# Another order for a fused attention and feed-forward kernel's written-out list of steps

## The chip, the cores and the metric

The kernel runs on one core of one Trainium2 chip. The metric is device microseconds of an execution; the figure for a kernel is the median of several runs. One further execution was recorded by the hardware profiler, and its durations are the ones used here.

## What is computed

Sliding-window attention with a linear distance penalty feeds a feed-forward layer. Cut to what matters:

```python
# q, k, v: 8 batches x 8 heads x 576 positions x 64
scores = q @ k.T / sqrt(64) - slope[h] * |i - j|     # only where 0 <= i - j < 128
attn   = exp(scores - max) / sum                     # per row
x      = (attn @ v)  ->  4608 tokens x 512
h      = x @ w_in                                    # 512 x 2048
out    = (h * sigmoid(beta * h)) @ w_out             # 2048 x 512, float32 out
```

## The kernel before

Everything lives in one function. It allocates its buffers, defines one small function for each kind of step, and then walks through one string, `PLAN` (line 18 on), of 1,300 words. Each word is a step: a name, sometimes a dot and the engine that does it (`p` GpSimd, called POOL in the profile; `v` VectorE, DVE; `a` ScalarE, ACT; `s` the SyncE queue, SP), and numbers. The loop at the end (lines 716 to 719) calls the function for each word in order:

```python
for step in PLAN.split():
    name, *at = step.split(":")
    name, _, eng = name.partition(".")
    STEPS[name](*([ENGINES[eng]] if eng else []), *map(int, at))
```

So the list is a written-out order of the program. Every engine and every queue executes its own instructions strictly in the order in which the list has them; between engines only semaphores hold, for data and for buffers that are reused. Nothing reorders afterwards. Whether two neighbours of the list on different engines run at the same time is decided when they run.

The work comes in 8 batches of 576 tokens (five blocks of 128, 128, 128, 128 and 64 rows) for attention and in 9 groups of 512 tokens for the feed-forward layer. The steps that matter here:

- `k`, `q` (line 315) and `gk`, `gq`, `gv` (line 306) load float32 inputs by SP into one of 14 staging buffers (`fst`). A load reuses a buffer, so it also waits for the cast that read it.
- `ck`, `cq`, `cK`, `cQ`, `cv` cast such a buffer to bf16 (all on line 205, `move`), into `bst` (4 buffers) or, for v, straight into the matmul operand `vs`. From batch 3 on v comes by a casting DMA of POOL, `pv` (line 342).
- `w1:n` and `w2:n` (lines 350 and 354) load a quarter of each weight matrix by POOL's casting DMA: `w2:n` brings rows 512n to 512n+511 of `w_out`.
- Batches 0 and 1: `Rk`, `Rq` transpose on TensorE (line 369), `rk`, `rq` copy the result out of PSUM, `A`, `B` are scores (lines 410 and 421), `EA`, `EB` exponentials (line 431), `VA`, `VB` the products with v (line 453), `nA`, `nB` the division (lines 437 and 438), `XP` the transposition for the next layer (line 464), `xc` its copy. `z` is an idle matmul (line 209), `fr`, `ft`, `fl` build constants.
- Batches 2 to 7: `D:b:s` (line 500) transposes block s of q and k by a DMA of SP into `qkT`; `S:b:m:p` are scores (line 522; half m = 0 needs blocks 0 to 2, half 1 all five), `E` the exponential (line 531), `M` the mask factor (lines 261 and 275), `V:b:s` the product with v (lines 574 and 577), `n` the division (lines 585 and 586), `XD` (line 620) the transposing DMA of SP that writes `XT`, the input of the next layer.
- `H:g:j` (line 632; in pieces `h`) is column block j of the first matrix product of group g, four matmuls of 512 columns into one bank of PSUM; `a:g:j` (line 640) its activation on ScalarE, `d:g:j` (line 645) the gating product on VectorE, which frees the bank and writes `gT`.
- `O:g:i:n` (line 655) is a quarter of the second product for 128 tokens, four matmuls; quarter n reads `w2:n` and columns 4n to 4n+3 of `gT`. `oc` (lines 677 and 679) evicts the result, `st` (line 684) stores it. The very last 128 tokens go in two halves (`OL` line 666, `lc`, `ls`).

The last number of each TensorE step is one of the 8 PSUM banks, so the list also decides which earlier result must have been evicted before a step can start.

Of the kernel before, what the change touches and what calls it, by code (L numbers as in the profile page):

```python
# [18 lines left out]
k.s:0:2 const ck.a:0:2 k.s:0:0 k.s:0:1 q.s:0:0 beta:4 k.s:1:0 ck.p:0:0 cq.v:0:0 ones ck.a:0:1 z:2:2  # L19
q.s:0:1 ck.a:1:0 z:2:1 q.s:0:2 q.s:0:3 Rk:0:0:3 Rk:0:1:6 z:1:4 z:1:2 k.s:1:3 gv.s:0:1 k.s:0:3  # L20
cq.v:0:1 Rk:0:2:0 Rk:1:0:1 rk.a:0:0 Rq:0:1:2 cq.v:0:2 rq.a:0:1 Rq:0:2:3 q.s:1:0 q.s:1:1 ck.p:1:3
ck.p:0:3 rq.a:0:2 rk.v:0:1 rk.v:0:2 Rq:0:0:4 B:0:1:6:0 rk.v:1:0 rq.a:0:0 B:0:0:4:0 A:0:2:2:1 EB:0:1
MB:0:1 cv.p:0:1 fr:2 cq.v:1:0 cq.a:0:3 A:0:0:6:1 EB:0:0 EA:0:2 z:2:0 gv.s:0:0 EA:0:0 B:0:2:0:1
cv.p:0:0 Rk:0:3:5 MB:0:0 fr:6 A:0:1:2:1 Rq:0:3:4 Rk:1:3:6 rq.v:0:3 rk.a:0:3 B:0:3:4:1 EA:0:1 EB:0:2
cq.v:1:1 EB:0:3 w1:0 Rq:1:1:7 rk.v:1:3 VA:0:0:3 VA:0:1:0 Rq:1:0:2 VA:0:2:6 A:0:3:4:1 nA:0:0 order
rq.v:1:1 gv.s:0:3 rq.a:1:0 cv.p:0:3 gv.s:0:2 B:1:0:1:0 k.s:1:1 q.s:1:3 cv.p:0:2 w1:1 nA:0:1 nA:0:2
VB:0:2:7 EA:0:3 VB:0:3:5 nB:0:2 ck.a:1:1 VB:0:1:4 VB:0:0:3 Rk:1:1:0 A:1:0:6:1 EB:1:0 nB:0:0 cq.p:1:3
q.s:1:2 nB:0:1 cq.p:1:2 rk.a:1:1 k.s:1:2 EA:1:0 XP:0:2:3 XP:0:0:2 w1:2 VA:0:3:4 gq.s:0:4 xc.a:0:0
nB:0:3 nA:0:3 Rq:1:3:1 XP:0:1:0 xc.v:0:2 A:1:1:5:1 rq.a:1:3 XP:0:3:1 pad ck.p:1:2 EA:1:1 A:1:3:3:1
B:1:1:6:0 xc.a:0:1 xc.a:0:3 h:0:0:5:0:3 EB:1:1 fr:7 fr:5 fr:4 EA:1:3 MB:1:0 H:0:2:1 gv.s:1:2  # L30
h:0:0:5:3:4 h:0:1:7:0:3 H:0:3:2 Rq:1:2:3 h:0:1:7:3:4 Rk:1:2:6 MB:1:1 a:0:2 a:0:3 d:0:2 fr:3 gv.s:1:1
fr:1 rk.v:1:2 a:0:0 H:0:7:1 gv.s:0:4 gk.s:0:4 H:0:6:4 H:0:4:6 gv.s:1:0 d:0:3 d:0:0 fr:0 cQ.a:0:4
fl:0 a:0:7 rq.a:1:2 cv.p:1:2 A:1:2:2:1 a:0:6 d:0:7 a:0:4 H:0:10:5 gv.s:1:3 H:0:5:0 gk.s:1:4 a:0:1
H:0:8:1 d:0:6 EA:1:2 d:0:4 a:0:10 w1:3 a:0:5 ft cK.p:0:4 cv.p:0:4 d:0:1 cv.p:1:0 a:0:8 cv.a:1:1
B:1:2:2:1 d:0:10 EB:1:2 H:0:9:5 VA:1:2:6 gq.s:1:4 d:0:5 d:0:8 gv.s:2:4 gv.s:2:1 gk.s:2:0 VA:1:0:1
TT:0:7 H:0:11:4 cv.p:1:3 a:0:9 VA:1:1:0 a:0:11 nA:1:2 tt.v:0 nA:1:0 d:0:9 B:1:3:6:1 EB:1:3 VB:1:2:5
SCT:0:1 nA:1:1 w2:0 VB:1:0:0 gv.s:1:4 gq.s:2:0 VA:1:3:3 d:0:11 ECT:0 gk.s:2:1 cK.p:2:1 VB:1:1:4
gk.s:2:2 cv.p:1:4 H:0:14:7 nB:1:2 nB:1:1 h:0:15:1:0:2 cQ.a:1:4 gq.s:2:4 gk.s:2:4 a:0:14 cK.a:1:4
VB:1:3:4 w2:1 h:0:15:1:2:4 XP:1:1:2 nA:1:3 MCT:0 PV:0:0:6 nB:1:0 XP:1:2:3 PV:0:1:5 gq.s:2:2 cQ.p:2:2
xc.a:1:1 d:0:14 XP:1:0:0 xc.a:1:0 xc.a:1:2 TT:1:2 nV:0:1 nV:0:0 nB:1:3 a:0:15 H:0:12:7 H:0:13:0  # L40
tt.v:1 w2:2 X:0:4:3 a:0:13 XP:1:3:4 x.v:0:4 d:0:13 xc.a:1:3 SCT:1:5 H:1:7:2 ECT:1 a:1:7 H:1:14:0
d:0:15 a:0:12 fl:2 d:1:7 H:1:9:6 H:1:12:1 a:1:12 d:0:12 gq.s:2:1 gq.s:2:3 d:1:12 H:1:3:4 H:1:5:5
H:1:4:1 a:1:3 a:1:9 H:1:1:3 H:1:10:2 a:1:5 d:1:3 H:1:0:7 a:1:4 a:1:14 d:1:4 w2:3 a:1:1 a:1:10
cK.v:2:2 O:0:0:0:4 d:1:5 d:1:14 d:1:1 cQ.v:2:0 cQ.p:2:1 cv.p:2:4 d:1:10 cK.v:2:0 D:2:0 d:1:9
H:1:15:0 H:1:2:1 gq.s:3:1 D:2:2 a:1:2 a:1:0 H:1:13:5 cv.v:2:1 cQ.a:2:4 O:0:2:0:2 H:1:6:3 O:0:2:1:2
H:1:8:6 O:0:0:1:4 O:0:0:2:4 d:1:0 a:1:6 a:1:13 cK.a:2:4 gk.s:2:3 D:2:1 d:1:2 d:1:13 MCT:1 d:1:6
gv.s:2:0 O:0:2:2:2 O:0:3:0:3 gq.s:3:0 H:1:11:7 a:1:8 a:1:15 a:1:11 d:1:8 cQ.v:2:3 cv.p:2:0 d:1:15
gk.s:4:0 cQ.p:3:1 cK.v:2:3 d:1:11 O:0:0:3:4 O:0:2:3:2 O:0:3:1:3 D:2:4 D:2:3 S:2:0:0:0 S:2:0:1:5
oc.v:0:2 O:1:0:0:2 O:1:0:1:2 gv.s:2:3 E:2:0:1 E:2:0:0 gk.s:3:4 st.s:0:2 O:0:3:2:3 S:2:0:2:6 oc.v:0:0
S:2:0:3:4 PV:1:1:0 gk.s:3:0 E:2:0:3 O:1:0:2:2 E:2:0:2 gq.s:3:2 nV:1:1 fl:4 gv.s:2:2 M:2:0:3 M:2:0:2  # L50
O:0:3:3:3 fl:3 oc.v:0:3 S:2:1:3:4 E:2:1:3 M:2:0:1 fl:1 S:2:1:2:0 S:2:1:0:6 E:2:1:0 O:1:0:3:2
oc.a:1:0 M:2:1:3 E:2:1:2 S:2:1:1:4 M:2:0:0 gq.s:3:4 cv.p:2:2 cQ.v:3:0 M:2:1:0 O:0:1:0:3 E:2:1:1
PV:1:0:6 O:0:1:1:3 gq.s:4:1 gk.s:3:2 gk.s:4:4 gq.s:3:3 V:2:0:0 nV:1:0 cQ.p:3:4 M:2:1:2 O:1:1:0:2
V:2:1:4 n:2:0 O:1:2:0:7 gk.s:3:1 O:1:2:1:7 n:2:1 cQ.p:3:2 M:2:1:1 O:1:1:1:2 X:1:4:6 XD:2:0 XD:2:1
cv.a:2:3 pv:3:1 V:2:2:0 n:2:2 XD:2:2 O:1:2:2:7 O:1:1:2:2 V:2:3:4 O:1:2:3:7 x.a:1:4 cK.v:3:4
O:0:1:2:3 cK.v:3:0 n:2:3 oc.a:1:2 O:0:1:3:3 O:1:1:3:2 cK.v:3:2 cK.v:3:1 gk.s:3:3 st.a:0:0 V:2:4:5
H:2:4:0 H:2:1:7 D:3:0 D:3:2 n:2:4 gq.s:4:2 H:2:10:4 a:2:1 a:2:4 oc.a:0:1 D:3:1 oc.v:1:1 gk.s:4:2
H:2:3:1 H:2:5:6 d:2:4 H:2:2:0 d:2:1 H:2:0:7 D:3:4 a:2:5 H:2:7:3 st.s:1:0 a:2:10 d:2:10 a:2:2 a:2:3
cQ.p:4:1 a:2:0 a:2:7 gq.s:4:0 cK.p:3:3 cQ.v:3:3 d:2:2 d:2:5 d:2:3 H:2:9:4 O:1:3:0:2 a:2:9 cQ.p:4:0
S:3:0:0:5 S:3:0:2:0 O:1:3:1:2 d:2:0 d:2:7 gk.s:5:4 D:3:3 st.a:0:1 O:1:3:2:2 E:3:0:0 E:3:0:2  # L60
S:3:0:1:6 d:2:9 S:3:0:3:3 H:2:6:5 gk.s:4:1 H:2:11:1 O:1:3:3:2 H:2:8:0 E:3:0:1 pv:3:2 E:3:0:3 a:2:6
S:3:1:1:6 a:2:11 a:2:8 XD:2:3 H:2:12:4 E:3:1:1 d:2:6 d:2:11 cK.p:4:2 pv:3:0 cQ.v:4:2 a:2:12 H:2:13:5
d:2:8 M:3:0:1 d:2:12 oc.v:1:3 cK.p:4:0 S:3:1:0:0 E:3:1:0 H:2:14:6 M:3:0:3 M:3:0:2 S:3:1:3:3 a:2:14
S:3:1:2:0 d:2:14 E:3:1:3 O:2:0:0:2 O:2:0:1:2 E:3:1:2 D:4:0 gq.s:4:3 H:2:15:7 M:3:1:3 st.p:0:3
cK.p:4:1 pv:3:4 M:3:0:0 cQ.p:4:3 pv:4:0 st.p:1:2 a:2:15 a:2:13 M:3:1:1 M:3:1:0 d:2:15 O:2:2:0:3
O:2:0:2:2 pv:3:3 V:3:0:0 O:2:1:0:6 n:3:0 cK.v:4:4 d:2:13 M:3:1:2 O:2:1:1:6 V:3:1:0 n:3:1 O:2:1:2:6
V:3:2:4 O:2:1:3:6 n:3:2 gk.s:4:3 D:4:1 D:4:2 gq.s:4:4 gk.s:5:3 cK.v:4:3 cQ.p:4:4 O:2:0:3:2 O:2:2:1:3
st.a:1:1 oc.a:2:1 S:4:0:1:6 pv:4:1 S:4:0:3:4 S:4:0:2:0 E:4:0:1 O:2:2:2:3 E:4:0:3 O:2:3:0:7 E:4:0:2
XD:2:4 XD:3:0 XD:3:2 XD:3:1 oc.v:2:0 D:4:4 D:4:3 O:2:2:3:3 V:3:3:4 V:3:4:0 n:3:3 O:2:3:1:7 oc.v:2:2
O:2:3:2:7 n:3:4 H:3:2:4 H:3:0:2 a:3:2 S:4:0:0:5 d:3:2 a:3:0 gq.s:5:2 gq.s:5:0 M:4:0:1 H:3:7:0  # L70
E:4:0:0 d:3:0 a:3:7 O:2:3:3:7 H:3:1:5 d:3:7 oc.a:2:3 a:3:1 S:4:1:2:2 S:4:1:0:0 M:4:0:2 st.s:2:0
cQ.p:5:2 S:4:1:1:6 gk.s:5:1 E:4:1:0 d:3:1 E:4:1:1 H:3:6:4 H:3:4:5 a:3:6 E:4:1:2 H:3:3:1 XD:3:4
M:4:0:3 M:4:0:0 V:4:0:6 H:3:9:0 a:3:4 d:3:6 n:4:0 V:4:1:3 gq.s:5:1 XD:3:3 H:3:5:2 gk.s:5:2 pv:4:2
st.s:1:3 gq.s:5:3 H:3:12:7 gq.s:7:4 gk.s:5:0 XD:4:0 cK.a:5:1 a:3:3 n:4:1 a:3:9 M:4:1:0 H:3:8:3
XD:4:1 d:3:4 a:3:8 S:4:1:3:5 H:3:15:4 cK.p:5:2 E:4:1:3 d:3:3 pv:4:3 pv:4:4 a:3:12 d:3:9 H:3:14:0
a:3:14 a:3:5 d:3:8 pv:5:1 M:4:1:2 d:3:14 d:3:5 H:3:10:3 H:3:11:1 H:3:13:5 a:3:10 a:3:13 gq.s:5:4
H:4:1:2 H:4:4:6 H:4:2:0 cQ.p:5:3 a:3:11 cK.a:5:0 cQ.a:5:1 M:4:1:3 d:3:12 d:3:13 O:3:1:0:5 H:4:0:7
cQ.v:5:0 d:3:11 a:4:1 cK.p:5:3 cQ.p:5:4 D:5:2 a:3:15 st.s:2:1 a:4:2 gq.s:6:2 a:4:0 d:3:10 D:5:0
d:4:1 d:4:2 cK.v:5:4 gk.s:6:0 D:5:1 d:4:0 a:4:4 O:3:1:1:5 H:4:7:1 H:4:3:0 M:4:1:1 d:3:15 d:4:4 a:4:7
pv:5:4 H:4:5:7 a:4:3 O:3:0:0:4 O:3:0:1:4 O:3:1:2:5 V:4:4:2 a:4:5 O:3:1:3:5 d:4:3 d:4:7 d:4:5  # L80
S:5:0:1:6 S:5:0:0:0 st.s:2:3 gk.s:7:1 n:4:4 D:5:4 D:5:3 gk.s:6:2 V:4:2:2 E:5:0:1 oc.v:3:1 n:4:2
O:3:0:2:4 E:5:0:0 gq.s:7:2 V:4:3:6 n:4:3 O:3:0:3:4 S:5:0:2:2 E:5:0:2 pv:6:1 S:5:1:0:0 pv:5:0 XD:4:4
gk.s:7:0 oc.a:3:0 pv:5:2 S:5:0:3:5 st.a:3:0 E:5:1:0 gq.s:6:4 st.p:2:2 H:4:6:7 O:3:2:0:3 O:3:3:0:2
O:3:2:1:3 st.p:3:1 E:5:0:3 S:5:1:1:4 S:5:1:2:0 E:5:1:1 a:4:6 O:3:3:1:2 O:3:2:2:3 E:5:1:2 M:5:0:0
M:5:0:2 M:5:0:3 M:5:0:1 V:5:0:4 O:3:3:2:2 XD:4:2 gq.s:6:3 O:3:3:3:2 n:5:0 V:5:1:5 XD:5:0 H:4:8:1
XD:4:3 O:3:2:3:3 a:4:8 n:5:1 oc.a:3:2 H:4:9:5 a:4:9 oc.a:3:3 H:4:11:6 H:4:10:3 H:4:12:2 d:4:8
M:5:1:2 d:4:9 a:4:11 a:4:12 d:4:11 d:4:6 H:4:13:1 H:4:15:4 XD:5:1 a:4:15 a:4:10 O:4:1:0:7 H:4:14:5
a:4:14 a:4:13 O:4:1:1:7 d:4:12 cQ.v:6:2 d:4:10 d:4:15 gk.s:6:1 d:4:13 gq.s:6:1 gk.s:6:4 gq.s:7:0
d:4:14 H:5:2:0 a:5:2 M:5:1:1 d:5:2 H:5:8:2 H:5:10:3 H:5:1:5 O:4:1:2:7 S:5:1:3:0 a:5:8 d:5:8 cK.a:6:2
# [660 lines left out]
```

## Time and profile before

| what | value |
|---|---|
| runs | 323.64, 324.43, 325.98 us; median 324.43 |
| the profiled execution | 323.59 us |
| its span, first to last instruction | 321.8 us |
| granted TensorE clock, mean over the span | 0.994 |
| busy, ScalarE and VectorE | 58% and 62% |
| DMA: read from HBM, written to it | 36.71 MB, 9.44 MB |
| last matmul ends | 318.3 us |

A line of a timeline has the start, the time it took, the engine (SPq is SP's queue of DMA issues), the line of the code, what is written and read and how many instructions it merges; in square brackets stands the idle time before it and what ended it. A line of the stretches has the stretch, its length, and for TensorE, its weight loads, VectorE, ScalarE and POOL the busy time with the number of instructions, then the granted clock, the busy share of the DMA engines and GB/s. A line of the waits has the waiting engine and line, what it waited for, the sum in us, how often, and the longest.

### The profile page before, as it was taken

The page shows a single profiled execution, that of the slowest core. Times are in us where ns is not written, and L with a number is a line of the kernel's source. Part 1 is how long each engine was busy: PE and PEld are TensorE (multiplying, and loading weights), DVE is VectorE, ACT ScalarE, POOL GpSimd, SP SyncE. Part 2 cuts the span into 40 slices and gives each one's busy share as a digit, 9 for nine tenths or more (in the row PEclk, how much of TensorE's full clock was granted, in tenths as well). Part 3 has the DMA queues.
Part 4 walks back from the last instruction along what each step waited for, and adds up shares of the span by engine and source line. Part 5 has one row for each costly group of instructions (what it writes and reads, how often), then busy time and mean ns, then how long its engine had stood idle before and what let it go on. Part 6 is the DMA issues. An engine that isn't in the chain of part 4 may idle for free.

```text
span 321.8 us, 5879 instructions
## 1 busy us (share of the span) xinstructions
PE 307.9 (96%) x2218; PEld 152.2 (47%) x2257; DVE 198.1 (62%) x391; ACT 186.3 (58%) x278; POOL 62.9 (20%) x101
## 2 busy tenths in 40 slices
PE   8899999979989999899999999999999999999995
PEld 3464554434544445354455444544544544444543
DVE  4789886843856494588755645752876536865102
ACT  7999786615407854479565664746469324773010
POOL 2372404101301631242050143112000000000000
PEclk9999999998999999999999999999999999999999
DMA  7999999999999999999999899599651134000023
GB/s 243 281 250 199 194 202 187 180 210 223 201 167 233 189 201 172 202 226 179 210 152 230 149 178 138 71 174 182 84 103 35 51 70 152 1 33 2 33 83 147
DMA packets 152684, 50.01 MB, mean 155 GB/s; under 512 B 140288, under 2 KB 148752, under 8 KB 152656
## 3 DMA queue, kind: packets, MB, share of 16 engines
q1 hardware_dynamic: 122512, 37.24, 63.2%
q0 software_dynamic: 28384, 9.51, 27.4%
q10 hardware_dynamic: 1760, 2.89, 2.5%
q8 instruction: 17, 0.28, 0.4%
q14 instruction: 11, 0.09, 0.1%
HBM read 36.71 MB, written 9.44 MB: 143 GB/s over the span
## 4 chain that ended last, share of the span: by engine, by line
PE 74%; DMA 12%; SPq 6%; DVE 2%; POOL 2%; issue 2%; ACT 1%; POOLq 0%; ACTq 0%
PE PS L632 33%; PE PS L655 30%; DMA XT<-xn 6%; PE PS L522 4%; DMA fst<-in_q_dram 3%; DMA fst<-in_k_dram 2%; SPq L500 2%; PE PS L577 2%; SPq L315 2%; PE PS L574 2%; SPq L306 1%; DMA qkT<-bst 1%; PE PS L666 1%; DVE bst L205 1%; PE PS L453 1%
## 5 line engine op out<-in xcount | busy, mean ns | idle before, releaser
L632 PE MATMUL PS<-XT,W 128*128 128x512 bf16 x558 | 132.3, 379 | 3.5 <-DMA XT<-xn 2.3
L640 ACT ACTIVATE sig<-PS,beta_h 128x512 bf16<-128x512 f32 x144 | 94.4, 688 | 68.6 <-PE PS L632 61.9
L655 PE MATMUL PS<-W,gT 128*128 128x512 bf16 x540 | 131.7, 382 | 1.4 <-issue 0.5
L645 DVE SCALAR_TENSOR_TENSOR gT<-sig,PS 128x512 bf16<-128x512 bf16 x144 | 94.0, 683 | 57.1 <-ACT sig L640 56.7
L632 PEld LDWEIGHTS <-W 128*128 128x128 bf16 x576 | 54.2, 98 | 66.9 <-issue 4.2
L655 PEld LDWEIGHTS <-gT 128*128 128x128 bf16 x560 | 52.6, 98 | 61.5 <-issue 3.7
L531 ACT ACTIVATE pt<-PS 128x1024 bf16<-128x1024 f32 x48 | 47.0, 1023 | 22.5 <-PE PS L522 22.1
L205 POOL CAST bst<-fst 128x512 bf16<-128x512 f32 (+1 forms) x33 | 21.0, 644 | 102.4 <-DMA fst<-in_q_dram 36.1
L677 ACT ACTIVATE osb<-PS 128x512 f32<-128x512 f32 (+1 forms) x20 | 11.3, 576 | 33.6 <-PE PS L655 24.0
L342 POOL DMA_DIRECT2D vs<-in_v_dram x25 | 21.1, 847 | 26.4 <-PE PS L577 26.4
L684 POOL DMA_DIRECT2D out_dram<-osb x9 | 5.1, 576 | 88.5 <-DVE osb L679 84.0
L679 DVE TENSOR_SCALAR osb<-PS 128x512 f32<-128x512 f32 x17 | 11.4, 686 | 17.2 <-PE PS L655 17.2
L586 DVE TENSOR_TENSOR xn<-PS,zb 128x512 bf16<-128x512 f32 (+1 forms) x30 | 20.7, 690 | 1.0
L275 DVE TENSOR_TENSOR pt<-pt,fall 128x1024 bf16<-128x1024 bf16 x24 | 16.0, 684 | 4.8 <-ACT pt L531 4.8
L585 DVE RECIPROCAL zb<-PS 128x8 f32<-128x8 f32 (+1 forms) x30 | 6.1, 202 | 19.0 <-PE PS L577 18.4
L205 DVE CAST bst<-fst 128x512 bf16<-128x512 f32 (+1 forms) x28 | 12.6, 455 | 7.1 <-DMA fst<-in_q_dram 2.7
L577 PE MATMUL PS<-vs,pt 128*128 128x65 bf16 x240 | 16.9, 193 | 0.0
L261 DVE TENSOR_TENSOR pt<-pt,falls 128x1024 bf16<-128x1024 bf16 x24 | 16.3, 700 | 0.9 <-ACT pt L531 0.8
L522 PE MATMUL PS<-qkT 64*128 64x256 bf16 (+2 forms) x240 | 14.9, 250 | 2.0 <-DMA qkT<-bst 1.8
L577 PEld LDWEIGHTS <-pt 128*128 128x128 bf16 x240 | 14.6, 97 | 3.5 <-DVE pt L275 0.2
L431 ACT ACTIVATE pt<-PS 128x1024 bf16<-128x1024 f32 (+1 forms) x16 | 14.3, 931 | 0.8 <-PE PS L421 0.6
L522 PEld LDWEIGHTS <-qkT 64*128 64x128 bf16 x240 | 8.7, 94 | 12.6 <-issue 12.1
(73 smaller groups left out, 171.9 us busy)
## 6 DMA issues: line engine op xcount, KB each, us to landing
fst<-in_k_dram SPq DMA_DIRECT2D x32, 256.0 KB, 4.8
fst<-in_q_dram SPq DMA_DIRECT2D x32, 256.0 KB, 5.2
out_dram<-osb SPq DMA_DIRECT2D x16, 256.0 KB, 3.1
fst<-in_v_dram SPq DMA_DIRECT2D x12, 256.0 KB, 6.2
vs<-in_v_dram POOLq DMA_DIRECT2D x20, 128.0 KB, 6.3
out_dram<-osb ACTq DMA_DIRECT2D x10, 256.0 KB, 3.0
out_dram<-osb POOLq DMA_DIRECT2D x9, 256.0 KB, 4.0
W<-in_moe_w_in_dram POOLq DMA_DIRECT2D x4, 512.0 KB, 9.0
```

The lines of the kernel that those rows point to most:

```text
L205: (nc.scalar.copy if eng is nc.scalar else eng.tensor_copy)(out=out, in_=in_)
L261: nc.vector.tensor_tensor(out=pt[:], in0=pt[:], in1=falls[:, 2 * p : 2 * p + 2], op=ALU.mult)
L275: nc.vector.tensor_tensor(out=x, in0=x, in1=bass.AP(tensor=t.tensor, offset=t.offset, ap=[list(t.ap[0]), [P, 4], [0, 2], [1, P]]), op=ALU. ...
L342: return nc.gpsimd.dma_start(out=VS[b % 2][0:rows, sb, :, 0:D], in_=v[b, :, P * sb : P * sb + rows, :].rearrange("h p d -> p h d"))
L522: nc.tensor.matmul(o, lhsT=qk[64 * e : 64 * e + 64, 1, p, P * kb : P * kb + P], rhs=qk[64 * e : 64 * e + 64, 0, p, P * kb : P * kb + nq], ...
L531: nc.scalar.activation(out=pt[:], in_=held.pop(("S", b, m, p)), func=ACTF.Exp, scale=qscale)
L577: nc.tensor.matmul(o, lhsT=weights(b, qb, h, 0), rhs=vs[:, qb, h, 0 : D + 1], start=qb == 0, stop=True, skip_group_check=True)
L586: nc.vector.tensor_tensor(out=xn[0:nq].rearrange("p (g h) d -> p g h d", g=2), in0=pv[0:nq, :, :, 0:D], in1=zs[0:nq].broadcast_to([nq, 2, ...
L632: nc.tensor.matmul(hps, lhsT=W1[:, c, bass.ts(j, P)], rhs=XT[:, c, c0 : c0 + TOKG], start=(c == 0), stop=(c == NDM - 1),)
L640: nc.scalar.activation(out=sig[:], in_=hps, func=ACTF.Tanh, scale=beta_h[:, j : j + 1])
L645: nc.vector.scalar_tensor_tensor(out=gts[g][:, j, :], in0=held.pop(("H", g, j))[:], scalar=1.0, in1=hs.pop((g, j)), op0=ALU.add, op1=ALU.mult)
L655: nc.tensor.matmul(ops_, lhsT=gT[:, j, i * P : i * P + P], rhs=W2[:, j, :], start=(j == 0), stop=(j == NFF - 1),)
```

## The change

Only the string `PLAN` changes; no function does. The new list has the same steps, each once, but another order from the first word on: the loads, the casts, the TensorE steps, the stores and the queues' DMAs all stand elsewhere. In a few words, as it was described: the list of steps made anew from batch 1's loads to group 2, with other places for the first transposes of batch 2 and the last blocks of W2; the text of the list differs beyond that stretch too. The bank numbers are other ones, and a part of the casts, evictions and stores moved to another engine:

| steps | before | after |
|---|---|---|
| input casts on VectorE, POOL, ScalarE | 29, 45, 21 | 16, 52, 27 |
| evictions `oc` on ScalarE, VectorE | 18, 17 | 19, 16 |
| stores of whole blocks on SP, ScalarE, POOL | 16, 10, 9 | 15, 8, 12 |

Cut to the stretches that the prediction speaks of:

```diff
-k.s:0:2 const ck.a:0:2 k.s:0:0 k.s:0:1 q.s:0:0 beta:4 k.s:1:0 ck.p:0:0 cq.v:0:0 ones ck.a:0:1 z:2:2
...
-VB:1:3:4 w2:1 h:0:15:1:2:4 XP:1:1:2 nA:1:3 MCT:0 PV:0:0:6 nB:1:0 XP:1:2:3 PV:0:1:5 gq.s:2:2 cQ.p:2:2
-xc.a:1:1 d:0:14 XP:1:0:0 xc.a:1:0 xc.a:1:2 TT:1:2 nV:0:1 nV:0:0 nB:1:3 a:0:15 H:0:12:7 H:0:13:0
-tt.v:1 w2:2 X:0:4:3 a:0:13 XP:1:3:4 x.v:0:4 d:0:13 xc.a:1:3 SCT:1:5 H:1:7:2 ECT:1 a:1:7 H:1:14:0
...
-H:1:4:1 a:1:3 a:1:9 H:1:1:3 H:1:10:2 a:1:5 d:1:3 H:1:0:7 a:1:4 a:1:14 d:1:4 w2:3 a:1:1 a:1:10
-cK.v:2:2 O:0:0:0:4 d:1:5 d:1:14 d:1:1 cQ.v:2:0 cQ.p:2:1 cv.p:2:4 d:1:10 cK.v:2:0 D:2:0 d:1:9
-H:1:15:0 H:1:2:1 gq.s:3:1 D:2:2 a:1:2 a:1:0 H:1:13:5 cv.v:2:1 cQ.a:2:4 O:0:2:0:2 H:1:6:3 O:0:2:1:2
-H:1:8:6 O:0:0:1:4 O:0:0:2:4 d:1:0 a:1:6 a:1:13 cK.a:2:4 gk.s:2:3 D:2:1 d:1:2 d:1:13 MCT:1 d:1:6
...
+const ones q.s:0:1 cq.a:0:1 k.s:0:1 ck.p:0:1 q.s:0:0 beta:1 q.s:0:2 k.s:0:0 k.s:0:2 order cq.v:0:0
...
+nA:0:0 VB:0:2:4 EB:1:0 nB:0:2 Rq:1:1:5 Rk:1:1:2 VB:0:1:3 VB:0:0:6 rq.v:1:1 rk.a:1:1 VA:0:3:1 nB:0:1
...
+gq.s:3:4 h:0:15:1:0:2 a:0:14 cQ.p:2:2 cv.a:0:4 XP:1:2:5 XP:1:1:4 VA:1:3:6 H:0:13:0 d:0:14 nA:1:3
...
+a:0:12 a:1:7 a:1:14 w2:0 gk.s:4:0 H:1:3:5 d:0:12 H:1:0:1 H:1:13:4 H:1:12:7 H:1:10:0 d:1:14 a:1:1
+cQ.a:2:3 d:1:1 a:1:3 cK.a:2:3 a:1:0 a:1:12 d:1:7 d:1:3 a:1:10 H:1:8:5 a:1:13 cK.v:2:0 d:1:0 H:1:9:6
+w2:1 w2:3 H:1:4:1 H:1:2:2 d:1:13 w2:2 d:1:10 d:1:12 a:1:9 a:1:8 a:1:4 d:1:4 cK.a:2:2 H:1:11:0
+cv.a:1:4 cK.a:2:1 cQ.a:2:0 d:1:8 fl:2 O:0:3:0:3 a:1:2 cQ.a:2:1 d:1:9 H:1:15:1 D:2:0 H:1:6:7
+O:0:0:0:5 O:0:0:1:5 O:0:3:1:3 O:0:2:0:4 H:1:5:6 a:1:15 a:1:11 a:1:6 D:2:1 gv.s:2:3 d:1:11 d:1:6
+D:2:2 O:0:3:2:3 PV:1:1:7 gv.s:2:0 D:2:3 O:0:0:2:5 cK.p:2:4 cQ.p:2:4 O:0:3:3:3 O:0:2:1:4 a:1:5
...
```

In the new list all four `w2` steps follow POOL's cast `cQ.p:2:2` with no other POOL step between them; in the old list `w2:0` stands two steps of POOL ahead of `w2:1`, and `w2:2`, `w2:3` after `cQ.p:2:2`. The transposes stand in the order 2:0, 2:1, 2:2, 2:3, 2:4 instead of 2:0, 2:2, 2:1, 2:4, 2:3.

## The prediction

> **What bounds the kernel now.** I read the page first, then the waits of the matmul engine, the stretches around its longest wait, the timelines of SP and POOL there, and last the chain at the end.
>
> ```profile
> span 321.8 us, 5879 instructions
> PE 307.9 (96%) x2218; PEld 152.2 (47%) x2257; DVE 198.1 (62%) x391; ACT 186.3 (58%) x278; POOL 62.9 (20%) x101
> ```
>
> TensorE is the bound: 96% busy, the next engine 62%. I priced every PE step by its start-to-start time in the trace: 215.5 ns for a 512-column matmul (an H or O step of four: 0.86 us), 56 ns for a transposing one, 29 to 30 ns for a 128x65 one, 0.27 us for an S step of half 0, 0.475 us for a V step. Both lists hold the same steps, so both sum to 296.25 us. The last matmul of before ends at 318.3, so 22.0 us went to waits and to slow matmuls. The sum of what stands before a step in the list I call its place, and its real time less its place its offset. It is 9.2 us at the first H step (24.05 us), 11.3 at 46 us and still at 66 us, 16.8 at 97 us, 18.7 at 133 us, 20.3 at 205 us, 21.4 at 224 us and 22.0 from 263 us to the end. The largest step lies between 66 and 97 us.
>
> ```profile
> PE PS L632 <- DMA XT<-xn: 2.3, 3, 0.9
> PE PS L522 <- DMA qkT<-bst: 1.8, 1, 1.8
> ```
>
> ```profile
> 69.00:71.00 2.00, 0.40 (x2) 0.00 (x0) 0.99 (x3) 0.00 (x0) 0.00 (x0) 1.00 1.10 209
> 71.00:73.00 2.00, 1.76 (x12) 0.91 (x13) 1.23 (x3) 1.11 (x2) 0.26 (x1) 0.75 1.22 248
> 73.00:75.00 2.00, 1.78 (x6) 0.62 (x5) 0.00 (x0) 0.82 (x1) 0.91 (x2) 0.50 1.41 186
> ```
>
> The first S step of batch 2 (L522) waits 1.84 us for the transposing DMAs of batch 2 (D steps, L500), from 69.4 to 71.24 us; then the granted clock (the column after the engines) falls to 0.50 and eight O matmuls run at 427 ns. Lost: 2.0 + 8 x 0.211 = 3.7 us.
>
> ```profile
> 58.63 1.45 SPq L500 DMA_TRANSPOSE qkT<-bst  x1
> 60.18 0.54 SPq L306 DMA_DIRECT2D fst<-in_q_dram  x1
> 60.84 5.49 SPq L500 DMA_TRANSPOSE qkT<-bst  x1
> 66.37 0.58 SPq L306 DMA_DIRECT2D fst<-in_k_dram  x1
> 67.07 1.41 SPq L500 DMA_TRANSPOSE qkT<-bst  x1
> ```
>
> ```profile
> 50.70 0.74 POOL L354 DMA_DIRECT2D W<-in_moe_w_out_dram  x1
> 54.15 0.61 POOL L205 CAST bst<-fst 128x512 bf16<-128x512 f32 x1 [2.71 <-DMA fst<-in_q_dram]
> 54.70 1.48 POOL L354 DMA_DIRECT2D W<-in_moe_w_out_dram  x2
> ```
>
> Why the D steps are late: D:2:0 is issued at 58.63 and lands at 66.7 (8.1 us; the median D takes 4.0), D:2:2 keeps SP for 5.49 us instead of about 1.4, and D:2:1 stands behind it and lands at 71.1. Meanwhile the last W2 blocks move: issued at 50.7, 54.7 and 55.4, landed at 58.8, 62.2 and 65.75.
>
> **The change part by part.** *Amount of work.* Nothing is added or removed: the same loads, matmuls and exponentials, in another order on every queue, in other PSUM banks. Of the input casts 13 leave VectorE (29 to 16), 7 for POOL (45 to 52) and 6 for ScalarE (21 to 27). TensorE's work covers them, with the three at 62%, 20% and 58%; a cast that a D step waits for uncovered costs its 0.43 to 0.61 us.
>
> *Start, to the first H step.* Loads land 0.7 to 1.2 us apart in before (3.77, 4.52, 5.78 ... 17.29 for the 16th, 18.97 for the 17th), and nothing in the new order of their casts stops them sooner. The new list loads V's block 2 as 17th instead of 16th, so its cast ends at about 19.7 (before 17.96). VB:0:2 waits for it; from there to the first H the list holds 4.9 us of PE work, on ScalarE eight operations of 0.52 to 0.69 us from Rk:1:1 on, giving H at 25.0 to 25.5, at place 15.4: offset 9.6 to 10.1 against 9.2. W1's first block is issued at 15.7 in both (landed 24.1). Batch 1's V block 0 then lands one load earlier, about 34.4 against 35.3, which gives some back. I take +0.2 us (0 to +1.0).
>
> *W2.* In the new list POOL issues all four W2 blocks together, after its cast of q 2:2 (36th load; 39th before). From 36.6 us (27th load, in both) I count bytes: before moved 2.6 MB in 10.1 us, 0.26 MB/us. To q 2:2 the new list needs 2.0 MB of loads and the rest of the fourth W1 block, 0.6 MB: 10 us, so about 46.5. Then 4 blocks of 1.05 MB and 1.2 MB of loads at 0.26 to 0.30 MB/us (w2:2 to w2:3 was 3.5 us for one block): the last lands at 64.5 to 67. The list issues w2:3 third and w2:2 last, but O:0:3:2, at place 53.8, that is 53.8 + 11.4 = 65.2 us, needs w2:2. The wait is 0 to 1.9 us; I take 1.0, the middle. All matmuls queue behind it.
>
> *First transposes of batch 2.* D:2:0 is issued behind its ScalarE cast at about 59.5, D:2:1 next, and both meet the W2 traffic till about 66 as in before. The S step stands at place 60.0 instead of 58.1 and 1.0 later for W2: 72.4 us. As in before, D:2:1 and D:2:2 land 2 to 5 us after the traffic stops, at 69 to 71: no wait. D:2:4 (three issues of about 1.5 us further, 4 us to land) comes at about 76, the half that needs it (place 62.9) at 75.3: 0.7 us. So 3.7 us go and 1.0 + 0.7 come, -2.0 us.
>
> [...] The row shows clock 0.50 after 1.84 us; the waits of 0.81 and 0.94 us at 94.95 and 132.15 are followed by 216 ns matmuls. The row decides: I take 3.7, and for new waits of 1 us no slow matmuls; from about 1.8 us I add 1.7.
>
> *XT's transposes (L620).* V steps of a group's last blocks to its first H. Group 3: 7.2 us of PE work in place of 8.7 after V:3:2; in before three transposes were issued from 122.1 and landed at 128.1, 130.0, 132.0, two us apart, and PE lost 1.1. Now the third would be issued 2.1 us after its V and land 6.5 us later: 1.4, +0.3 us. Group 6: its four blocks' covers are 12.7, 12.9, 16.0 and 27.9 instead of 9.6, 13.3, 19.0 and 24.0, and XD:5:2, which landed last among those at 221.5 (stood behind other SP work till 215.5), is far ahead in SP's order: its loss of 0.7 us goes. Groups 2, 4, 5, 7 and 8 stay within 2 us of cover and above their chains.
>
> *Banks.* Three V or S steps now follow 0.86 us after the O whose eviction frees their bank (V:2:2, V:4:3, S:7:0:0); the closest such before is 1.34. A ScalarE eviction is 0.58 us and its start may be blocked by a 1.02 us exponential or, for V:2:2, by a V cast whose load is issued late: 0.5 + 0.2 + 0.2. Of four small losses of before (0.31, 0.29, 0.35, 0.36 us) I let half go: +0.25.
>
> *Tail.* Both lists end with the same half-width block; 3.5 us follow the last matmul in before (copy 0.38, then the store). The last stores are spread over as many queues: no change.
>
> **Sum:** +0.2 - 2.0 + 0.3 - 0.7 + 0.25 = -1.95 us. The span, 321.8, becomes 319.9; the execution, 1.8 us longer than the span for what lies around it, 323.59 - 1.95 = 321.6. The median of the runs, 324.43, is 0.84 above the profiled one: 322.5 us.
>
> **Rivals.** *Slower: W2 comes too late.* One mechanism: the q 2:2 load, hence all of W2, is later than 46.5. POOL's cast of it stands behind those of batch 1's late loads, and in before POOL stood idle for 11.65 us for just such a load. Each us later is a us of wait at O:0:3:2, and from 1.8 us on the clock adds 1.7. With wait W the change is W - 1.95 (no S wait then): slower from W = 2, by over 1% from W = 5.2, a q 2:2 at 50.7. At 54.0, where it landed in before, W = 8.5 and the time is 331. For it: w2:1 stands at place 31.4 of the old list, 42 us with the offset there, and came at 50.7, because the cast ahead of it on POOL waited for a load. Against: the loads are fewer ahead of it and no W2 among them.
>
> *Faster: W2 and the transposes both in time.* If the traffic runs at 0.30 MB/us, W2 is in by 65 and the D steps by 71: -3.7 whole, sum -3.65 (320.8), and without the bank and group 3 terms 320.2. For it: the S step stands 1.9 us later in the list. Against: of the three D steps it needs, only one landed within 2 us of W2's end in before.
>
> *Nothing gained: the wait only moves.* The S step is covered, but many small new waits (ten bank reuses of 0.3 us, or the first H at offset 10.2) eat it: 324.4, perhaps 326. All reuse distances are redrawn, and those under 2.5 us are 135 against 126.
>
> **How the numbers follow.** My forecast 0.40, spread 321 to 324; faster rival 0.25 (318.5 to 321); the wait that moves 0.15 (324 to 327); W2 late 0.20 (326 to 332). The likeliest is 322.5. Leaving out under 0.1 at each end gives 318.5 to 329. About 1% (3.2 us) is what a measurement of this kernel can tell from no change: faster is below 321.2, slower above 327.7 us. Faster: the rival's 0.25 and 0.05 of mine, 0.30. Slower: 0.18 of W2 late and 0.02 of the moved wait, 0.20. Between: 0.50.
>
> **What would show it.** Right: no DMA wait of L522 over 1 us at 70 to 78 us and granted clock 1.00 there; a wait of L655 for W of 0 to 2 us near 65; offset at the first H 9.2 to 10.2; the L632 wait near 220 gone, the one near 130 still there. Wrong: q 2:2 landing after 48, the four L354 issues after 49, clock under 1.00 near 66 to 70, or an offset at the end above 22.

## The result, and the profile after

| | before | after |
|---|---|---|
| median of 13 runs | 324.64 us | 321.93 us |
| lowest to highest | 323.40 to 326.10 | 320.10 to 324.84 |
| profiled execution, its span | 323.59, 321.8 us | 321.93, 320.1 us |
| last matmul ends | 318.3 us | 316.9 us |

The ratio is 0.9929, with a 95% interval of 0.9904 to 0.9954: 0.7% less time. Medians here are over all executions, while the ratios leave out executions counted as disturbed (8 of the 29 of before that stand beside the experiments, none of those above), so a ratio is not just the quotient of two medians. The two profiled executions differ by 1.66 us only, the medians by 2.7: that of before is 1.05 us below its own median, that of after stands on its median.

The page of after has nearly the same amount of work as that of before, with TensorE still the bound:

```profile
span 320.1 us, 5872 instructions
PE 307.8 (96%) x2220; PEld 153.0 (48%) x2257; DVE 193.9 (61%) x376; ACT 190.5 (60%) x286; POOL 68.7 (21%) x111
```

The waits of TensorE in after, its longest first (waiting engine and line, what it waited for, sum in us, times, longest):

```profile
PE PS L655 <- DMA W<-in_moe_w_out_dram: 2.8, 2, 2.6
PE PS L369 <- DVE bst L205: 1.3, 1, 1.3
...
PE PS L655 <- issue: 1.0, 6, 0.2
```

The two rows that led the list of before are gone: no wait for `XT` (2.3 us in three) and none of L522 for the transposes of batch 2 (1.84 us). In their place stands one wait of 2.64 us for the last block of W2, on `O:0:3:2`. What it costs is seen in the stretches of after around it (columns as before):

```profile
66.00:68.00 2.00, 0.04 (x1) 0.00 (x0) 0.00 (x0) 0.69 (x1) 0.00 (x0) 1.00 1.36 113
68.00:70.00 2.00, 1.32 (x4) 0.49 (x4) 0.00 (x0) 0.00 (x0) 0.53 (x1) 0.62 1.35 207
70.00:72.00 2.00, 2.00 (x13) 0.96 (x13) 0.95 (x3) 0.00 (x0) 0.63 (x2) 0.53 1.41 154
72.00:74.00 2.00, 1.95 (x10) 0.94 (x10) 2.00 (x6) 0.60 (x1) 0.00 (x0) 1.00 1.31 254
```

TensorE stands from 66 to 68.67 us, and then its clock is granted at 0.62 and 0.53 until 72 us: seven matmuls at about 427 ns instead of 216, another 1.5 us. POOL's timeline of after shows why W2 is late:

```profile
50.42 0.61 POOL L205 CAST bst<-fst 128x512 bf16<-128x512 f32 x1 [11.64 <-DMA fst<-in_q_dram]
50.97 2.96 POOL L354 DMA_DIRECT2D W<-in_moe_w_out_dram  x4
```

POOL idled 11.64 us for the load of q 2:2, which landed at 50.27; only then were the four blocks issued, and they landed at 58.93, 62.34, 65.33 and 68.63 us, 3.0 to 3.4 us apart. `w2:2`, the one that `O:0:3:2` reads, is the last of them.

So the stretch that the forecast put its gain in shows none. The table below, worked out from the traces as the prediction's offsets were, shows where the two lists drift apart, and has the four experiments of the next section beside them. Places are us of TensorE work, of 296.25.

```
place           20     44    80    107   115   134   188   206   263
before         9.2   11.3  16.8   17.6  18.75  19.5  20.3  21.4  22.0
after         10.9   12.0  17.25  17.9  18.1   18.6  19.7  20.0  20.65
w2swap        11.4   14.1  15.7   16.35 17.3   18.5  19.6  19.85 20.5
oldstart      12.9   14.8  17.3   17.9  18.4   19.0  20.1  20.4  21.0
w2early       10.6   16.0  19.2   19.8  20.0   20.5  21.75 22.0  22.7
oldw2         11.6   13.8  20.4   21.2  21.25  24.4  26.4  27.1  27.7
```

After is behind before up to place 107 and ahead only from 115 on. Its gains lie at the three places where before waited for `XT`: place 78 (group 2, 0.7), 112 (group 3, 0.95) and 190 to 206 (group 6, 0.8).

TensorE's timelines at the first H steps of groups 3 and 6, before:

```profile
132.15 1.02 PE L632 MATMUL PS<-XT,W 128*128 128x512 bf16 x4 [0.94 <-DMA XT<-xn]
221.56 1.68 PE L632 MATMUL PS<-XT,W 128*128 128x512 bf16 x7 [0.53 <-DMA XT<-xn]
```

and after, with no idle time ahead of them:

```profile
130.93 2.32 PE L632 MATMUL PS<-XT,W 128*128 128x512 bf16 x10
219.82 1.89 PE L632 MATMUL PS<-XT,W 128*128 128x512 bf16 x8
```

For group 3 SP's timelines show what changed. Before, from 115 to 132 us, the L620 row only:

```profile
120.18 6.14 SPq L620 DMA_TRANSPOSE XT<-xn  x4
```

After, the same stretch:

```profile
122.17 4.56 SPq L620 DMA_TRANSPOSE XT<-xn  x3
```

Four issues in a row before, three after. The fourth is `XD:2:4`, a transpose of group 2 that in before stood right ahead of group 3's three and landed at 127.7, with theirs at 128.1, 130.0 and 132.0 behind it; TensorE waited until 132.15. In after it is issued at 109.8, group 3's land at 125.8, 130.2 and 130.5, and the first H of group 3 starts at 130.93 without a wait. In group 6 the last to land in before was `XD:5:2`, at 221.51; in after it lands at 199.1, and the last of that group's at 214.7.

### The profile page after: what moved, and what is told of

Its sections match the earlier page's. It is cut to its first block, busy times and chain, and to the rows that moved or that the text cites. A ratio compares the mean times of both kernels' runs of the same rounds, so it can differ in the third digit from the quotient of the medians.

```text
span 320.1 us, 5872 instructions
## 1 busy us (share of the span) xinstructions
PE 307.8 (96%) x2220; PEld 153.0 (48%) x2257; DVE 193.9 (61%) x376; ACT 190.5 (60%) x286; POOL 68.7 (21%) x111
## 4 chain that ended last, share of the span: by engine, by line
PE 84%; DMA 8%; ACT 2%; SPq 2%; issue 1%; DVE 1%; POOL 1%; POOLq 0%; DVEq 0%
PE PS L655 37%; PE PS L632 33%; DMA W<-in_moe_w_out_dram 5%; PE PS L522 4%; DMA fst<-in_q_dram 3%; PE PS L577 2%; PE PS L574 2%; SPq L306 2%; PE PS L666 1%; PE PS L369 1%; ACT pt L431 1%; PE PS L421 1%; PE PS L410 1%; PE PS L453 1%; POOL W L354 1%
## 5 line engine op out<-in xcount | busy, mean ns | idle before, releaser
L205 POOL CAST bst<-fst 128x512 bf16<-128x512 f32 (+1 forms) x43 | 27.2, 650 | 96.2 <-DMA qkT<-bst 34.4
L677 ACT ACTIVATE osb<-PS 128x512 f32<-128x512 f32 (+1 forms) x21 | 12.0, 577 | 43.6 <-PE PS L655 42.4
L684 POOL DMA_DIRECT2D out_dram<-osb x12 | 6.8, 565 | 105.8 <-ACT osb L677 93.8
L342 POOL DMA_DIRECT2D vs<-in_v_dram x25 | 21.1, 847 | 22.1 <-PE PS L577 11.6
L679 DVE TENSOR_SCALAR osb<-PS 128x512 f32<-128x512 f32 x16 | 10.9, 686 | 18.9 <-PE PS L655 18.9
L577 PE MATMUL PS<-vs,pt 128*128 128x65 bf16 x240 | 16.5, 193 | 0.0
L577 PEld LDWEIGHTS <-pt 128*128 128x128 bf16 x240 | 14.4, 97 | 3.3
L522 PE MATMUL PS<-qkT 64*128 64x256 bf16 (+2 forms) x240 | 14.9, 250 | 0.0
L574 PE MATMUL PS<-vs,pt 128*128 128x65 bf16 x192 | 14.4, 193 | 0.0
L574 PEld LDWEIGHTS <-pt 128*128 128x128 bf16 x192 | 13.1, 97 | 2.2
```

The lines of the kernel that those rows point to most:

```text
L205: (nc.scalar.copy if eng is nc.scalar else eng.tensor_copy)(out=out, in_=in_)
L342: return nc.gpsimd.dma_start(out=VS[b % 2][0:rows, sb, :, 0:D], in_=v[b, :, P * sb : P * sb + rows, :].rearrange("h p d -> p h d"))
L522: nc.tensor.matmul(o, lhsT=qk[64 * e : 64 * e + 64, 1, p, P * kb : P * kb + P], rhs=qk[64 * e : 64 * e + 64, 0, p, P * kb : P * kb + nq], ...
L574: nc.tensor.matmul(o, lhsT=weights(b, qb - 1, h, 1), rhs=vs[:, qb - 1, h, 0 : D + 1], start=True, stop=False, skip_group_check=True)
L577: nc.tensor.matmul(o, lhsT=weights(b, qb, h, 0), rhs=vs[:, qb, h, 0 : D + 1], start=qb == 0, stop=True, skip_group_check=True)
```

## The experiments

The theory after the result (A) was the forecast's own: the stretch of W2 and batch 2's transposes is where the time is, so the wait that has come up there is time still to be had. The rivals were that this wait only moves, and that the start is what changed the time. All four kernels ran on the same chip, beside the same runs of the kernel before (median 324.19 us of 29); after itself was not run again beside them, so its 321.93 is to be read with the 324.64 that before had there. They leave nothing of the computation out.

**w2swap: the last two W2 blocks of the new list change places.**

```diff
-w2:1 w2:3 H:1:4:1 H:1:2:2 d:1:13 w2:2 d:1:10
+w2:1 w2:2 w2:3 H:1:4:1 H:1:2:2 d:1:13 d:1:10
```

> The new list with one pair exchanged: w2:2 is issued third and w2:3 fourth. Theory A (the order of the last W2 blocks causes the 2.6 us wait at 66 us and the seven slow matmuls after it): w2:2 lands near 65.3 and w2:3 near 68.6, O:0:3:2 starts without a wait, O:0:3:3 (two steps later) waits at most 1 us, the granted clock stays 1.00 there, and the S step waits at most 1 us: 2.5 to 3.5 us faster than the new list, about 319. Rival B (the transposes of batch 2 bound this stretch whatever W2 does): the wait moves to the S step, and the time stays within 1 us of 321.9.

Measured: 322.60 us (321.12 to 324.42, 12 runs), ratio to before 0.9981 (0.9945 to 1.0016). Its stretches, at the place of the wait:

```profile
66.00:68.00 2.00, 2.00 (x11) 0.94 (x10) 0.69 (x1) 0.56 (x2) 0.00 (x0) 1.00 0.93 122
68.00:70.00 2.00, 1.95 (x17) 1.03 (x16) 0.98 (x3) 0.57 (x1) 1.16 (x2) 1.00 1.13 234
70.00:72.00 2.00, 2.00 (x11) 0.88 (x9) 2.00 (x6) 0.60 (x1) 0.00 (x0) 1.00 1.24 189
```

The wait is gone and the clock stays at 1.00: from place 44 to 80 this kernel loses 1.6 us, after 5.25. It had come to place 44 later than after by 2.1 us, although the two lists are the same up to there (its trace has two waits for casts of v on POOL, 2.1 us in sum, that after's does not have), and so it is 1.55 us ahead of after at place 80. Yet its span is 320.0 us against 320.1, and its median is not lower. The time is that of rival B, but the wait did not move to the S step. The table says where the lead goes: 0.75 us between places 107 and 115, 0.7 between 115 and 134. The first of these is in its waits:

```profile
PE PS L628 <- DMA XT<-xn: 0.6, 1, 0.6
```

The wait ends at 130.12 us and is for group 3's transposes (here line numbers are 4 lower). The input of the first of the three was ready at 120.6 instead of 122.1, but SP issued it at 121.95 instead of 122.17, behind a load, a store and a load that stand ahead of it, and the three landed at 129.1, 129.7 and 130.0 against 125.8, 130.2 and 130.5. The second part lies at 150 to 154 us, where H steps of group 3 wait for their banks: the gating products that free them stand on VectorE behind mask factors of 1.07 and 1.49 us (0.69 and 0.68 in after). So the lead of 1.55 us is given back by 154 us.

**w2early: all four W2 blocks of the new list right behind POOL's cast of q 1:4, in the order 0, 1, 2, 3.**

```diff
 cQ.p:1:4
+w2:0 w2:1 w2:2 w2:3
...
-w2:0
...
-w2:1 w2:3
...
-w2:2
```

> The new list with all four W2 blocks issued in the order 0, 1, 2, 3 right after POOL's cast of q of batch 1's last block, some 12 us earlier (near 39 us instead of 51). Theory A: W2 is in before it is needed, no wait of L655 for W; but the q and k loads of batch 2 share the DMA engines with it and land later by up to the time of four blocks at 0.26 MB/us, 16 us, so their casts, D steps and the S step get late: 319 if the loads catch up, up to 325 if the S step waits. Rival B (the transposes bound it in any case): S waits over 2 us here and the time is 324 or more.

Measured: 323.93 us (321.94 to 325.49, 12 runs), ratio 1.0026 (0.9997 to 1.0054): the gain of the change is gone. W2 is issued at 41.9 to 44.1 and is all in at 60.05. But the inputs of batch 2 now share the DMA engines with it: k 2:3, issued at 42.1, lands at 56.86, in 14.7 us (in after: issued 41.3, landed 47.73, in 6.4). ScalarE stands 3.8 us for that load, because the cast is ahead of the activations in its order, and waits again, 3.2 us, for q 2:0. The first of the two:

```profile
56.88 0.62 ACT L201 CAST bst<-fst 128x512 bf16<-128x512 f32 x1 [3.80 <-DMA fst<-in_k_dram]
```

The gating products come late, the banks come free late, and TensorE waits at 56.9 and 70.4 us, 2.0 us each. It waits neither for W2 nor in the S step; the loss comes through the banks, which neither theory had named. Place 80 is reached 1.9 us later than in after, and the lateness stays to the end (22.7 against 20.65).

**oldw2: the old list, with the last three W2 blocks right behind the first.**

```diff
-w2:0
+w2:0 w2:1 w2:2 w2:3
```

> The list of before with w2:1, w2:2 and w2:3 moved to right behind w2:0 on POOL (near 38 us instead of 50.7 to 55.4). Theory A (the D steps were late because W2's last blocks shared the DMA engines with them): D:2:0 lands about 4 us after its issue instead of 8.1, the issue of D:2:2 takes under 2.5 us instead of 5.5, the S wait of 1.84 us and the eight slow matmuls go: 3 to 4 us faster than before, about 321, less what later loads of batch 2 cost. Rival (the D steps wait for their casts and the S step for the queue's order): the S wait stays, time within 1 us of 324.6 or slower.

Measured: 328.46 us (326.92 to 329.51, 6 runs), ratio 1.0168 (1.0125 to 1.0212). Slower by 4 us, where theory A had a gain of 3 to 4. Its waits:

```profile
PE PS L628 <- DVE gT L641: 3.9, 1, 3.9
PE PS L365 <- ACT bst L201: 2.5, 2, 1.6
PE PS L628 <- DVE bst L201: 2.0, 1, 2.0
```

The first comes from the same cause as in w2early. SP's timeline of oldw2:

```profile
42.92 3.26 SPq L302 DMA_DIRECT2D fst<-in_q_dram  x1
46.27 10.62 SPq L302 DMA_DIRECT2D fst<-in_k_dram  x2
56.98 0.96 SPq L302 DMA_DIRECT2D fst<-in_q_dram  x1
```

and VectorE's:

```profile
61.17 0.43 DVE L201 CAST bst<-fst 128x512 bf16<-128x512 f32 x1 [4.23 <-DMA fst<-in_k_dram]
61.52 1.28 DVE L641 SCALAR_TENSOR_TENSOR gT<-sig,PS 128x512 bf16<-128x512 bf16 x2
```

Two issues of loads keep SP for 10.6 us (5.1 in before). k 2:2 lands at 61.08 instead of 51.58; VectorE waits 4.23 us for it, the gating products behind the cast (L641) free TensorE's bank at 62.8, and TensorE has stood for 3.91 us. With seven matmuls at 427 ns after it, this makes 5.4 us, the step from 13.8 to 19.2 around place 44. The wait for the transposes of batch 2 did go: D:2:0 lands 3.3 us after its issue (8.1 in before), the issue of D:2:2 takes 1.4 us (5.5), and from there to place 80 this kernel loses 1.2 us, before 5.5. So theory A was right on what early W2 would save and wrong on what it costs. A further 3.7 us are lost at 152 to 158 us, where the list is the old one: a wait of 2.04 us for VectorE, then eight slow matmuls (clock 0.59 and 0.55 in the two stretches from 154 to 158 us). Why it comes in this kernel and not in before was not settled.

**oldstart: the old list up to the first H, the new one from there** (`EB:1:1` and `EA:1:3`, which the old list has later, stand at the seam).

```diff
-const ones q.s:0:1 cq.a:0:1 k.s:0:1 ck.p:0:1 q.s:0:0 beta:1 q.s:0:2 k.s:0:0 k.s:0:2 order cq.v:0:0
+k.s:0:2 const ck.a:0:2 k.s:0:0 k.s:0:1 q.s:0:0 beta:4 k.s:1:0 ck.p:0:0 cq.v:0:0 ones ck.a:0:1 z:2:2
...
```

> The start of the old list up to its first H step, then the new list without those steps. Theory A (the new start costs the 1.7 us by which the offset at the first H is larger, 10.9 against 9.2 us, and it stays to the end): 1.7 us faster than the new list, about 320.2, first H at 24 to 24.5 us. Rival C (what is lost early is given back, because W2 and the transposes at 66 us land at times set by the DMA): the wait at 66 us grows by about as much, and the time is within 0.6 us of 321.9.

Measured: 321.64 us (319.64 to 324.83, 12 runs), ratio 0.9932 (0.9902 to 0.9963): as fast as after. Putting the old start back gains nothing that can be measured. In the profiled execution it was not even early: the first H starts at 27.37 us, not at 24 to 24.5, and the first H steps stand at offset 12.9, two us behind after. A part of that is the seam, where a transposition (`Rk:1:2:7`) needs a bank that the exponential `EB:1:1` right ahead of it has to read first:

```profile
PE PS L365 <- ACT pt L427: 1.5, 1, 1.5
PE PS L651 <- DMA W<-in_moe_w_out_dram: 1.3, 1, 1.3
```

The wait of 1.50 us ends at 26.66 us, and the granted clock is 0.50 from 28.34 to 31.75. So the trace does not show what the old start is worth, but what becomes of lateness. At place 44 this kernel is 2.8 us behind after; at place 80 the two are level at 17.3. The wait for W2, the second row, gives back 1.3 us, since it is 1.33 us instead of 2.64, and no slow matmuls follow it (clock 1.00 from 68 to 72 us), which gives back 1.5. The last block lands at 69.87 us here and at 68.63 in after, 1.24 us later, while TensorE is 2.8 us later: the chain of transfers follows TensorE only in part, and the rest is made good by waiting less.

## Why the prediction was right, and where it was not

The number was right: 322.5 forecast, 321.93 measured, inside 318.5 to 329, and within 1% of before as the likeliest case had it. It was not right by its own steps: the term of W2 was 2.5 us too low and the three of XT together 2.05 us too high. That the two nearly cancelled was luck.

| term of the sum | forecast | after less before, from the two traces |
|---|---|---|
| start, up to place 44 | +0.2 | +0.7 |
| W2 and batch 2's transposes, place 44 to 78 | -2.0 | +0.5 |
| XT of group 2 | 0 | -0.7 |
| XT of group 3 | +0.3 | -0.95 |
| XT of group 6 | -0.7 | -0.8 |
| banks and the rest | +0.25 | -0.1 |
| tail (3.5 to 3.2 us) | 0 | -0.3 |
| sum | -1.95 | -1.65 |

*W2: the mechanism was right, its size was not.* The step that failed is "so about 46.5" for q 2:2; it landed at 50.27. The count took 0.6 MB of the fourth W1 block as still to come at 36.6 us. But this block was issued at 34.27 (31.83 in before) and landed at 41.88 instead of 38.89; k 2:0 behind it came 4.6 us after the load ahead of it, and the next seven loads 0.7 to 1.5 us apart. From q 2:2 on the chain is as described: four blocks, `w2:2` last. The load was 3.8 us late, and the wait became 2.64 us instead of 1.0, not 4.8: the last block landed 18.4 us behind q 2:2 instead of 19.7, and TensorE came to it 0.8 us later than forecast. By the prediction's own clock row (from about 1.8 us add 1.7) such a wait was to bring slow matmuls, and it did, 1.5 us. The wait for S that was put at 0.7 did not come, since S itself was 4 us later, at 76.6 us: the three transposes of its first half had landed by 73.0, and the other two, at 75.1 and 76.8, ahead of the second half at 79.0. With these three in the sum, -3.7 + 2.64 + 1.5 = +0.4, against +0.5 measured. Of the four signs of being wrong that the prediction named, three were seen (q 2:2 after 48, L354 after 49, clock under 1.00 at 66 to 70); the fourth, an offset above 22 at the end, was not.

The rival "W2 comes too late" thus described the event: with W = 2.64 it is past its own point of W = 2, from which it had the kernel slower. The kernel was not slower because the terms that the rival shared with the forecast were 2 us too high: those of XT.

*Group 3.* "The third would be issued 2.1 us after its V and land 6.5 us later": it landed 5.0 us after its issue, and the wait that was to stay went. The prediction looked at the cover from V to H and at the three transposes' own spacing, and not at what stands ahead of them on SP, which it did look at for group 6. In before that is `XD:2:4`; in after three transposes of batch 4 stand between it and them. No run changed that alone, but the six traces agree: from the first issue of the three to the last landing it takes 9.9 and 10.0 us where `XD:2:4` is issued right ahead (before, oldw2), and 7.9 to 8.3 in the other four. *Group 2* was left out as within 2 us of cover: its last transpose lands 0.8 us later than in before, but TensorE comes to the first H 2.2 us later (96.34 us against 94.14).

*The clock.* The prediction priced it from one row of before: a wait of 1.84 us was followed by slow matmuls at a clock of 0.50. After agrees, with 2.64 us. The four further lists show that length alone did not decide it: 1.50 us was followed by a clock of 0.50 in oldstart, 2.05 us in w2early was not; see the last section.

*The start.* The first H of before starts at 24.42 us in the trace, not at 24.05 as the prediction has it, so that the offset there is 0.37 us more than its 9.2; at place 20 it is 9.2. Nor is +0.7 from one trace each a measurement of the change: at place 20 the old start stands at 9.2 and 11.6 us in the two kernels that have it whole (before, oldw2), the new one at 10.9, 11.4 and 10.6 in three. The runs of oldstart show no gain from the old one.

What the runs show of the cause: it is not the start (after is behind there, and oldstart with the old start is as fast), and not the order in which W2 comes in the new list (w2swap takes its wait away at no gain). What is left are the transposes of groups 2, 3 and 6, whose waits make -2.45 us in the two traces; no run changed these alone. But the table has the gain where they are: from place 80 to 263 the four kernels with the new list lose 3.4 (after), 3.5, 3.7 and 4.8 us, the two with the old list 5.2 (before) and 7.3, of which 3.7 are the loss of oldw2 at 152 us. For group 6 the traces also agree among themselves: in before and in oldw2 the first H of the group starts 0.05 us after `XD:5:2` has landed, at 221.51 and 227.21; in the four with the new list that block lands at 198 to 200 us, the group's last at least 4.7 us ahead of its first H. Open is the other 1.05 us by which the medians differ more than the two profiled executions. That of before had the best start of all six, so before's usual execution may be late by more than its trace shows, where in after the wait for W2 takes such lateness up; this was not tested. No kernel that was run beats after beyond the spread: oldstart is 0.3 us lower, with nearly the same interval of its ratio.

## What to carry to other kernels

Before a wait is priced, ask what sets its end: when the end is the arrival of a chain of transfers, what is won or lost on the engine ahead of it can be levelled there (2.8 us in oldstart), and what is won by taking the wait away can be lost at the next such place, here a queue of transposes 60 us on. On a queue that issues in order, look for a transfer that nobody needs yet ahead of those that an engine is about to need; here the new list did so without a loss that the traces show, where weight loads moved ahead held back the inputs beside them (14.7 us for a load in w2early against 6.4 in after). Compare two versions by offsets at several places of the work, and take no difference from one trace each for the change's, since the same start stood 2.4 us apart in two executions.

## What the runs showed of the hardware that was not expected

*The clock after a wait.* Matmuls ran at half speed (427 ns instead of 216, granted clock 0.50) after waits of 1.84 us (before), 2.64 (after), 3.91 and 2.04 (both oldw2), seven or eight of them each time, and the clock was 0.50 after one of only 1.50 (oldstart). It was 1.00 after 1.33 us (oldstart) and after two waits of 2.00 and 2.05 us in w2early. So in these runs length alone did not decide.

What the traces show instead: the stretches at half speed last 3.41 us (72.00 to 75.41 in before, 68.48 to 71.89 in after, 28.34 to 31.75 in oldstart; one that begins behind the last matmul, at 321.17 in before and 321.07 in after, is cut off by the end of the trace), and the stretches at full speed between two changes are whole multiples of that (64.85 and 245.76 us in before, 58.03 and 249.17 in after, 88.75 in oldw2: 19, 72, 17, 73 and 26 times 3.413). So the changes of the clock that were recorded lie at the marks of a grid of 3.41 us, whose place differs from trace to trace. Cut at these marks, the stretches with the waits look like this; two of before, one each of after, oldstart and oldw2, two of w2early:

```profile
68.59:72.00 3.41, 1.57 (x13) 0.67 (x12) 1.99 (x4) 0.11 (x1) 0.00 (x0) 1.00 1.16 234
72.00:75.41 3.41, 3.19 (x8) 1.21 (x8) 0.23 (x1) 1.82 (x2) 1.17 (x2) 0.50 1.35 208
...
65.07:68.48 3.41, 0.97 (x5) 0.33 (x4) 0.00 (x0) 0.69 (x1) 0.00 (x0) 1.00 1.36 132
...
24.93:28.34 3.41, 1.54 (x14) 0.85 (x11) 2.99 (x7) 2.39 (x4) 0.72 (x3) 1.00 1.23 200
...
150.96:154.37 3.41, 1.37 (x7) 0.50 (x6) 3.31 (x7) 3.01 (x5) 0.00 (x0) 1.00 1.65 179
...
57.46:60.87 3.41, 1.89 (x8) 0.78 (x8) 1.70 (x3) 2.59 (x6) 0.00 (x0) 1.00 0.96 192
71.11:74.52 3.41, 2.06 (x16) 1.12 (x17) 2.33 (x6) 1.21 (x2) 1.17 (x2) 1.00 1.09 175
```

In before and after, from the first change of the clock on, each such stretch in which TensorE was busy for 1.57 us or less was followed by one at 0.50, and none with 2.42 us or more was. Of the other stretches above, those with 1.54 us (oldstart) and 1.37 us (oldw2) were followed by one at 0.50, those with 1.89 and 2.06 us (w2early) were not. The wait of before lay whole within one stretch; those of w2early were cut in two by a mark, at 57.46 and at 71.11 us. For a forecast, 1.7 us at a wait of about 2 us is a chance and not a price: with 1.7 us of idle time as the border, between the 1.84 us of before (3.41 less 1.57) and the 1.52 us of w2early (3.41 less 1.89), a wait of 2.0 us alone would lose the clock at about six in ten of the places where it can fall on the grid (an estimate from these figures).

*Loads behind weight blocks.* With four casting transfers of W2 issued within 2.2 us (w2early), a load of 256 KB issued among them took 14.7 us; in after, without them, the same load took 6.4. That it would be late was expected, by up to 16 us; it was 8.3.
